# Turning q on VectorE instead of TensorE in an attention and channel-mix kernel

## The chip, the cores and the metric

The kernel runs on one core of a Trainium2 chip. Its engines work side by side, each through its own queue in order: TensorE (PE in the profile; PEld are its weight loads), VectorE (DVE), ScalarE (ACT), GpSimd (POOL) and SyncE (SP); the last two mostly issue transfers (DMAs) here. The metric is the device time of one execution in microseconds (us). The kernel before takes 208.34 us, the median of 3 runs (207.24 to 208.76).

## The reference, cut to what matters

Eight batches, 8 heads, 576 tokens, head size 64, 32 memory slots. Per batch and head the keys and values are pooled into 32 memory rows by a softmax of `phi`, the queries attend to these rows, and the result goes, heads side by side, into a channel mix of width 512 (1024 inside):

```python
a = softmax(phi)                                  # over the 32 slots
k_m = einsum('bhsm,bhsd->bhmd', a, k); v_m = einsum('bhsm,bhsd->bhmd', a, v)
attn = softmax(q @ k_m.T / sqrt(64)) ; x = attn @ v_m   # x: batch, token, 512
x_prev = x shifted by one token (zeros first)
xk = mu_k * x + (1 - mu_k) * x_prev ; xr = mu_r * x + (1 - mu_r) * x_prev
out = sigmoid(xr @ w_r) * (relu(xk @ w_k)**2 @ w_v)
```

## The kernel before, in words

All products run in bf16 with sums in f32. `q`, `k`, `v` and the weights are cast by their loads, which GpSimd issues; `phi` comes as f32. A batch is loaded with 128 partitions as (2 groups of four heads) x (64 rows), and each partition holds 9 tokens of each of four heads (`NJ` = 9, `QR` = 64): token 9 p + j lies in partition p at place j. So a batch's 576 tokens are nine blocks of 64. In the kernel before, all that follows holds the blocks in the order `JT` (even ones, then odd ones), and `store` writes them back to their place.

An attention batch is made of small steps, each a closure in `attention(b)` under a short name:

- `exp`, `z`: exponentials of `phi` (line 225), their sums on PE (247) and the reciprocal `rz`. `kv`, `k`, `v`: pooled keys and values on PE, 36 or 72 small matmuls (237). `nk`, `hn`, `nv`: scaling by `rz`, out of PSUM (274, 281). `tk`, `ht`: the scaled keys are transposed on PE and copied to `kmT` by DVE (301, 305).
- q must have the head dimension on partitions before scores can be made. Batch 0 does this in `qh0`, `qh1` (`tr_q_rows`, 326: 18 transposes for each half of the rows, then one copy out of PSUM by DVE and one by ACT, 329). Batches 1 to 4 do it in `q0`, `q1` (`tr_q`, 339: 36 transposes on PE and four copies out of PSUM, 343; in batch 1 two of the copies go to ACT). Batches 5 to 7 use `qx` (`cross_q`, 315): two DMA transposes of q each, issued by SP, whose queue also issues the stores. After that of batch 5, `hold` puts a tiny copy of GpSimd's behind it, ahead of the later loads.
- `s0`, `s1` (`scores`, 358 and 362): for each group of four heads, eight matmuls of 64 rows by 32 columns with 320 or 256 tokens, into two PSUM tiles (`HALVES`), then two exponentials by ACT into `e`.
- `l0` to `l3` (`denom`, 372 and 377): sums over slots by one matmul, and the logarithm by ACT. `h*z`, `r*z` (382): exp of minus that. `y*`, `w*` (389): the product `at` on DVE.
- Batches 0 and 1 then make xk and xr directly (`nk0` to `nr1`, `mk*`, `mr*`: scaled values 432, matmuls `mxps` 288, copies out 449; `load_mu_b`, named `mub`, makes the `mu_m` they need). From batch 2 on, `x*` makes x (288, 401), `dd` its difference to the token before (413), and `k*d`, `r*d` mix them on DVE (423, 424). `before` says where a block of tokens finds its predecessor.

The channel mix runs over chunks of tokens: `c0` (576 tokens, two parts a and b) to `c8` with `keys` (520 PE, relu by ACT 524, square by DVE 528), `g:t` (`gate`, 543: tile t of 128 tokens, exponential by ACT 548) and `o:t` (`value`, 565; product with the gate on DVE 567, store by `store` on SP). Gates are held in pairs of tiles: after the odd tile, `gate` itself finishes the pair with ln(1 + x) and exp(-x) over 1024 columns (550, 551). Two pairs fit in SBUF.

The order is written out by hand in `PLAN`, one list of words for all engines: each word runs its step's instructions into the engines' queues at that point. `p:` words are loads of batch 0, of batch 1 and of the weights, `b:load` loads batch b + 2 in the order of `LOADS` into the buffers that batch b used; at most eight of GpSimd's loads are under way. All PSUM tiles come from one pool of eight. `busy` steps are idle matmuls.

Of the kernel before, what the change touches and what calls it, by code (L numbers as in the profile page):

```python
# [11 lines left out]
BF16 = mybir.dt.bfloat16  # L12
AF = mybir.ActivationFunctionType
# [5 lines left out]
    "p:q:0a 0:exp1 0:exp0 0:z 0:k0c p:q:0b 0:hn0 0:qh0 0:ht0 0:qh1 p:k:0b 0:s0 0:mub p:v:0a 0:l0 0:k1c 0:l1 0:hn1",  # L19
    "p:v:0b 0:mu 0:ht1 p:wr:0-4 0:h1z 0:v0c 0:s1 0:v1c p:phi:1 0:h0z 0:y1 0:l2 0:l3 0:nk0 0:y0 0:nk1 0:h3z 0:nr1",  # L20
    "p:wk:4-8 0:h2z 0:busy4 0:nr0 0:y3 0:y2 0:mr1 0:mr0 p:wk:0-4 0:mk1 1:exp g:2 g:0 0:mk0 g:3 1:z c0:2a c0:7b c0:6b",
    "c0:4a c0:1b p:k:1 p:q:1 c0:2b 1:k 1:nk c0:0b c0:7a c0:5b c0:3a c0:1a 1:q0 c0:3b 1:q1 1:tk c0:4b c0:0a 1:s0 p:v:1",
    "1:s1 1:v c0:6a 1:l1 1:nr1 1:l0 c0:5a p:wv:0-2 1:nk0 1:l2 p:wv:2-4 1:nk1 1:nr0 1:h1z 1:l3 0:load 1:y1 1:h2z 1:h0z",
    "1:h3z g:1 1:y3 o:3a o:2a 1:y2 1:y0 o:2b o:3b 1:mk1 o:1b 1:mk0 1:mr0 c1:5 1:mr1 c1:2 2:exp c1:6 c1:3 c1:1 c1:0",
    "1:load 2:z g:4 g:5 2:q1 2:q0 2:kv 2:nk o:0b 2:load o:1a 2:tk 3:exp 2:nv c1:7 2:s1 2:s0 c1:4 2:l2 o:0a 2:l1 3:z",
    "2:l0 2:r0z 2:w0 2:l3 2:r1z 2:w1 o:4 o:5 2:x0 3:kv 3:nk 3:nv g:6 3:tk 3:q0 3:q1 2:x1 2:dd 2:k0d g:7 g:8 3:s0",
    "2:k2d 3:s1 o:6 o:7 3:l0 2:r2d 3:l2 3:load 3:l1 2:r0d 3:l3 3:r1z c2:3 4:exp c2:2 c2:5 3:r0z 3:w1 c2:0 3:w0 c2:4",
    "c2:6 g:10 c2:1 4:z 3:x1 4:kv 4:nk 4:nv c2:7 3:x0 g:11 3:dd 4:q0 4:q1 4:tk 5:exp o:11 g:9 5:qx o:10 5:z 5:kv",
    "3:k0d 4:s1 3:k2d 4:s0 o:9 g:12 4:l3 5:nk 3:r0d 4:l2 c3:2 c3:6 5:nv 4:l0 4:l1 4:r1z 4:w1 c3:3 4:r0z 4:w0 5:tk",
    "c3:7 c3:4 3:r2d c3:0 c3:5 5:s0 5:hold 5:load 4:x1 o:8 c3:1 5:l1 4:x0 4:dd g:13 4:k2d 5:l0 g:14 o:13 4:load o:12",  # L30
    "7:exp 5:r0z 4:k0d g:16 5:w0 g:15 7:z 7:kv 5:s1 c4:5 7:qx c4:1 c4:4 6:qx 4:r0d 7:nv c4:0 c4:3 6:exp 5:l2 7:nk",
# [5 lines left out]
    "c7:4 c8:2 c8:7 g:28 g:29 c8:3 c8:0 c8:5 g:31 o:28 o:29 o:31 7:load g:32 o:30 g:33 g:34 g:35 o:32 o:33 o:34 o:35",  # L37
]

LOADS = {None: ("phi", "k", "v", "q"), 2: ("phi", "k", "q", "v")}  # L40
PRE = "k:0a id:"
SUMS = ()

# [577 lines left out]
```

## Time and profile before

| | |
|---|---|
| median of 3 runs | 208.34 us |
| the profiled execution | 208.79 us, its span 207.0 us |
| PE busy | 192.7 us (93% of the span) |
| ACT busy | 159.4 us (77%) |
| DVE busy | 133.9 us (65%) |
| POOL busy | 29.6 us (14%) |
| PE: keys L520, values L565, gates L543 | 66.9, 65.6 and 34.6 us |
| granted clock, mean | 0.998 |
| HBM read and written | 38.28 and 9.44 MB |

The page comes from one execution. Its span begins and ends with the first and last instruction, and the execution takes some 1.8 us more. Busy times of PE overlap where small tiles run beside each other, so that line sums can exceed what a group holds the engine. A group of instructions is given as line, engine, operation, the tiles written and read, the shape, the count, total busy time and mean, then the idle time just ahead of them and what ended it.

### The profile page before, as it was taken

The page shows a single profiled execution, that of the slowest core. Times are in us where ns is not written, and L with a number is a line of the kernel's source. Part 1 is how long each engine was busy: PE and PEld are TensorE (multiplying, and loading weights), DVE is VectorE, ACT ScalarE, POOL GpSimd, SP SyncE. Part 2 cuts the span into 40 slices and gives each one's busy share as a digit, 9 for nine tenths or more (in the row PEclk, how much of TensorE's full clock was granted, in tenths as well). Part 3 has the DMA queues.
Part 4 walks back from the last instruction along what each step waited for, and adds up shares of the span by engine and source line. Part 5 has one row for each costly group of instructions (what it writes and reads, how often), then busy time and mean ns, then how long its engine had stood idle before and what let it go on. Part 6 is the DMA issues. An engine that isn't in the chain of part 4 may idle for free.

```text
span 207.0 us, 5511 instructions
## 1 busy us (share of the span) xinstructions
PE 192.7 (93%) x2213; PEld 103.6 (50%) x2235; DVE 133.9 (65%) x360; ACT 159.4 (77%) x314; POOL 29.6 (14%) x46
## 2 busy tenths in 40 slices
PE   0489999999999999999999999999999999999992
PEld 0355577745655445544458654444444444444441
DVE  1236455884668996899594969767887856615232
ACT  3246999987968998979899977899968655686570
POOL 7644222201504000007400000000000000000000
PEclk9999999999999999999999999999999999999999
DMA  6999999999999999298999997832060215202525
GB/s 160 178 208 260 207 207 205 261 221 292 209 284 240 262 269 201 61 133 205 187 231 298 198 165 115 189 71 52 0 152 5 51 33 119 54 0 62 135 67 141
DMA packets 31641, 33.06 MB, mean 160 GB/s; under 512 B 9072, under 2 KB 26752, under 8 KB 31616
## 3 DMA queue, kind: packets, MB, share of 16 engines
q0 software_dynamic: 17392, 20.91, 54.2%
q1 hardware_dynamic: 13456, 10.96, 24.5%
q10 hardware_dynamic: 768, 0.85, 1.3%
q8 instruction: 17, 0.28, 0.5%
q14 instruction: 8, 0.07, 0.1%
HBM read 38.28 MB, written 9.44 MB: 231 GB/s over the span
## 4 chain that ended last, share of the span: by engine, by line
PE 89%; DMA 6%; issue 1%; POOL 1%; ACT 1%; DVE 0%; SPq 0%; POOLq 0%; DVEq 0%
PE pk L520 31%; PE pv L565 29%; PE pr L543 15%; DMA q<-in_q_dram 4%; PE kvps L237 3%; PE zps L372 2%; PE mxps L288 2%; DMA qT<-q 2%; PE scps L358 2%; PE nops L288 2%; PE qtps L339 1%; PE idle L195 1%; PE zps L247 1%; PE mub L200 1%; PE qtps L326 1%
## 5 line engine op out<-in xcount | busy, mean ns | idle before, releaser
L520 PE MATMUL pk<-xkT,wk 128*128 128x512 bf16 (+4 forms) x346 | 66.9, 340 | 0.4
L565 PE MATMUL pv<-wv,sq 128*128 128x512 bf16 (+1 forms) x322 | 65.6, 353 | 0.4
L524 ACT ACTIVATE rl<-pk 128x512 bf16<-128x512 f32 (+3 forms) x80 | 41.9, 560 | 9.9 <-PE pk L520 8.7
L528 DVE TENSOR_TENSOR sq<-rl 128x512 bf16<-128x512 bf16 (+5 forms) x104 | 32.3, 340 | 26.0 <-ACT rl L524 25.0
L565 PEld LDWEIGHTS <-sq 128*128 128x128 bf16 x328 | 31.4, 98 | 30.0 <-issue 0.5
L520 PEld LDWEIGHTS <-wk 128*128 128x128 bf16 x352 | 32.9, 98 | 26.5 <-issue 0.5
L567 DVE TENSOR_TENSOR o<-sg,pv 128x512 f32<-128x512 f32 (+1 forms) x41 | 24.9, 619 | 18.9 <-PE pv L565 14.1
L543 PE MATMUL pr<-wr,xrT 128*128 128x512 bf16 x134 | 34.6, 381 | 0.5
L548 ACT ACTIVATE sg<-pr 128x512 f32<-128x512 f32 x36 | 21.3, 611 | 12.3 <-PE pr L543 5.2
L543 PEld LDWEIGHTS <-xrT 128*128 128x128 bf16 x144 | 13.5, 98 | 15.4 <-ACT xrT L449 0.4
L550 ACT ACTIVATE sg<-sg 128x1024 f32<-128x1024 f32 x18 | 19.0, 1057 | 0.6
L551 ACT ACTIVATE sg<-sg 128x1024 f32<-128x1024 f32 x18 | 19.0, 1057 | 0.6
L401 ACT CAST x<-nops 128x320 bf16<-128x320 f32 (+1 forms) x48 | 15.8, 428 | 3.6 <-PE nops L288 3.6
L423 DVE TENSOR_SCALAR mu_d<-diff,mu 128x576 bf16<-128x576 bf16 x48 | 15.5, 364 | 0.1
L389 DVE TENSOR_TENSOR atn<-e,lz 128x576 bf16<-128x576 bf16 (+2 forms) x20 | 12.4, 635 | 4.0 <-ACT lz L382 3.8
L377 ACT ACTIVATE lz<-zps 128x320 f32<-128x320 f32 (+1 forms) x32 | 11.9, 420 | 1.6 <-PE zps L372 1.6
L362 ACT ACTIVATE e<-scps 128x320 bf16<-128x320 f32 (+1 forms) x32 | 11.0, 416 | 1.5 <-PE scps L358 1.5
L382 ACT ACTIVATE lz<-lz 128x576 f32<-128x576 f32 (+2 forms) x20 | 11.6, 600 | 0.2
L413 DVE TENSOR_TENSOR diff<-x 128x1024 bf16<-128x1024 bf16 (+1 forms) x18 | 9.0, 554 | 3.4 <-ACT x L401 3.4
L225 ACT ACTIVATE em<-ph 128x1152 bf16<-128x1152 f32 (+1 forms) x9 | 9.4, 1050 | 2.1 <-DMA ph<-in_phi_dram 2.1
L237 PE MATMUL kvps<-kv,em 64*32 64x128 bf16 (+1 forms) x720 | 9.3, 219 | 1.0 <-DMA kv<-in_k_dram 1.0
L424 DVE TENSOR_TENSOR xkT<-x,mu_d 128x1152 bf16<-128x1152 bf16 x12 | 9.1, 759 | 0.4
(66 smaller groups left out, 140.7 us busy)
## 6 DMA issues: line engine op xcount, KB each, us to landing
out_dram<-o SPq DMA_DIRECT2D x61, 128.0 KB, 2.4
ph<-in_phi_dram POOLq DMA_DIRECT2D x7, 576.0 KB, 20.8
kv<-in_k_dram POOLq DMA_DIRECT2D x7, 576.0 KB, 17.3
q<-in_q_dram POOLq DMA_DIRECT2D x7, 576.0 KB, 21.3
kv<-in_v_dram POOLq DMA_DIRECT2D x7, 576.0 KB, 18.8
out_dram<-o SPq DMA_DIRECT2D x18, 64.0 KB, 5.6
wk<-in_moe_w_k_dram POOLq DMA_DIRECT2D x2, 512.0 KB, 14.7
wv<-in_moe_w_v_dram POOLq DMA_DIRECT2D x2, 512.0 KB, 20.0
```

Source lines behind the costliest of these rows:

```text
L237: nc.tensor.matmul(kvps[c][g * M:(g + 1) * M], lhsT=em[ROWS[c], j, g, :], rhs=kv5[ROWS[c], parts, g, j, :], start=j == 0, stop=j == NJ - 1 ...
L401: nc.scalar.copy(st["x"][:, i, sl], pss[i])
L423: nc.vector.tensor_scalar_mul(t[:, i], st["d"][:, pr + i, :], mu1[:, o:o + 1])
L520: nc.tensor.matmul(pk[:, p0 - lo:p1 - lo], lhsT=wk_sb[:, di, fi * 128:(fi + 1) * 128], rhs=xk_T[:, di, p0 % RING:p0 % RING + p1 - p0], sta ...
L524: nc.scalar.activation(rl, pk, AF.Relu)
L528: nc.vector.tensor_mul(sq[:, fi, p:p + p1 - p0], rl[:, p0 - lo:p1 - lo], rl[:, p0 - lo:p1 - lo])
L543: nc.tensor.matmul(pr, lhsT=xr_T[:, di, c0:c0 + 128], rhs=wr_sb[:, di, :], start=(di == 0), stop=(di == ND - 1))
L548: nc.scalar.activation(sg[:, t % 2], pr, AF.Exp, scale=-1.0)
L550: nc.scalar.activation(sg, sg, AF.Ln, bias=1.0)
L551: nc.scalar.activation(sg, sg, AF.Exp, scale=-1.0)
L565: nc.tensor.matmul(pv[:, cols], lhsT=sq[:, fi, p:p + 128], rhs=wv_sb[:, fi, cols], start=(fi == 0), stop=(fi == NF - 1))
L567: nc.vector.tensor_mul(o[:, cols], gated[t // 2][:, t % 2, cols], pv[:, cols])
```

## The change

- q is turned by DVE, SBUF to SBUF. `turn_q` reads bf16 pairs as 32-bit words and transposes each 32x32 block of them: one instruction for two heads of each group (128 partitions, 576 words), for all batches from 1 on (`q0`, `q1`); in batch 0 one for each half of the rows (64 partitions, 1152 words; `qh0`, `qh1`). The transposes on PE, their copies out of PSUM, `cross_q` and `hold` go.
- A partition then holds a pair's place in the head dimension (32 pairs), for 32 rows of q, with both members of the pair side by side. So `norm_k` writes the keys with even and odd members of the head dimension apart, `tr_k` keeps them as two planes `h`, and `scores` sums over the two planes: matmuls of 32 rows by 32 columns with 288 tokens, four row groups (two head groups, two halves of the 64-row blocks), in four PSUM tiles of 288 columns where both head groups run in one step (`s`), or two tiles for one group (batch 0). The exponentials put the halves back in place: `e` has its nine blocks of 64 tokens in natural order.
- `JT` goes: blocks are in natural order, and `before` and `store` follow.
- The two last passes of a pair of gates are a step of their own, `sg:p` (`settle`), and either tile of a pair may come first.
- `LOADS` has one order for all batches, and `PLAN` is written anew. It also loads k's second half ahead of q in batch 0, and `wk`'s first half ahead of the second and of `wr`.

```diff
-    "p:q:0a 0:exp1 0:exp0 0:z 0:k0c p:q:0b 0:hn0 0:qh0 0:ht0 0:qh1 p:k:0b 0:s0 0:mub p:v:0a 0:l0 0:k1c 0:l1 0:hn1",
-    "p:v:0b 0:mu 0:ht1 p:wr:0-4 0:h1z 0:v0c 0:s1 0:v1c p:phi:1 0:h0z 0:y1 0:l2 0:l3 0:nk0 0:y0 0:nk1 0:h3z 0:nr1",
-    "p:wk:4-8 0:h2z 0:busy4 0:nr0 0:y3 0:y2 0:mr1 0:mr0 p:wk:0-4 0:mk1 1:exp g:2 g:0 0:mk0 g:3 1:z c0:2a c0:7b c0:6b",
-    "c0:4a c0:1b p:k:1 p:q:1 c0:2b 1:k 1:nk c0:0b c0:7a c0:5b c0:3a c0:1a 1:q0 c0:3b 1:q1 1:tk c0:4b c0:0a 1:s0 p:v:1",
-    "1:s1 1:v c0:6a 1:l1 1:nr1 1:l0 c0:5a p:wv:0-2 1:nk0 1:l2 p:wv:2-4 1:nk1 1:nr0 1:h1z 1:l3 0:load 1:y1 1:h2z 1:h0z",
-    "1:h3z g:1 1:y3 o:3a o:2a 1:y2 1:y0 o:2b o:3b 1:mk1 o:1b 1:mk0 1:mr0 c1:5 1:mr1 c1:2 2:exp c1:6 c1:3 c1:1 c1:0",
...
+    "0:exp0 p:k:0b 0:exp1 0:z p:q:0a 0:mu 0:k0c p:q:0b p:v:0b 0:k1c 0:hn0 0:hn1 p:v:0a p:wk:0-4 0:qh0 0:ht0 0:ht1",
+    "0:mub 0:qh1 0:s0 0:l0 0:l1 0:h1z 0:s1 0:h0z p:phi:1 0:v1c 0:nk1 0:v0c 0:y0 0:y1 0:l3 0:l2 0:h2z 0:busy3 0:nr1",
+    "p:wk:4-8 0:nk0 0:h3z 0:y2 0:y3 0:nr0 0:mk0 0:mr0 0:mk1 c0:3a 0:mr1 c0:2a p:wr:0-4 c0:2b p:k:1 c0:1b c0:5b c0:7b",
+    "1:exp c0:6b c0:7a g:3 g:2 c0:0a 1:z c0:4b c0:5a 1:k sg:1 1:nk g:1 1:tk p:q:1 1:q1 1:q0 c0:1a c0:4a c0:0b c0:3b",
+    "1:s p:v:1 c0:6a p:wv:0-2 1:l0 1:l1 1:h0z 1:l2 1:l3 1:v p:wv:2-4 1:h2z 1:nk0 1:nr1 1:nk1 1:y0 1:h1z 1:nr0 1:y2",
+    "1:h3z 1:y1 1:y3 g:0 0:load o:3a o:2a 1:mk1 1:mk0 o:3b c1:0 c1:5 1:mr0 c1:4 c1:2 1:load 2:exp o:2b c1:7 sg:0",
+    "1:mr1 g:5 g:4 sg:2 3:exp o:0b o:1a 2:z 2:kv 2:nk 2:q0 o:1b 2:tk 2:q1 o:0a 2:nv c1:1 c1:3 2:s g:7 c1:6 2:l1 2:l0",
+    "2:l2 2:l3 2:r0z 2:w0 2:r1z 2:w1 3:z o:4 6:load o:5 2:x0 3:kv 3:nk 2:x1 g:6 3:q0 3:q1 3:tk 2:dd 2:load 3:nv g:8",
+    "2:k0d 3:s sg:3 2:k2d o:7 2:r0d 4:exp 2:r2d 3:l1 3:l3 3:load 3:l0 3:l2 o:6 3:r0z c2:2 c2:4 3:r1z 3:w1 3:w0 c2:1",
+    "c2:0 g:11 c2:6 4:q0 g:9 c2:3 4:z 3:x1 c2:7 c2:5 3:x0 4:q1 sg:4 4:kv 4:nk 3:dd g:10 4:nv o:9 5:exp 3:k2d o:8 4:tk",
+    "sg:5 g:12 3:k0d o:10 5:q1 4:s 5:kv 3:r2d c3:5 3:r0d 4:l0 c3:1 5:q0 4:l1 c3:3 4:r0z 4:l2 5:z 5:nk 5:load c3:0",
+    "4:l3 5:nv 4:load c3:2 4:r1z c3:7 g:13 4:w0 sg:6 4:w1 5:tk c3:6 o:11 7:load 4:x0 c3:4 g:14 4:x1 7:q1 7:exp 7:q0",
+    "g:15 sg:7 4:dd o:13 o:12 7:z 5:s 7:kv 4:k0d 6:exp o:14 g:17 5:l2 4:r0d g:16 5:l0 5:l1 7:nk 4:k2d 5:l3 sg:8 5:r1z",
+    "7:nv o:15 6:q0 7:tk 5:w1 c4:2 c4:1 c4:0 c4:6 6:z 5:r0z 6:kv 6:nv 7:s 5:w0 6:nk c4:4 4:r2d c4:3 7:l2 c4:5 c4:7",
+    "7:l1 6:q1 7:l3 5:x0 o:17 5:x1 6:tk 5:dd g:18 g:19 7:l0 6:s o:16 sg:9 6:l1 6:l0 5:k2d 6:r0z 5:k0d 6:w0 5:r0d g:21",
+    "7:r1z o:19 7:r0z 6:l3 7:w1 g:20 6:l2 c5:5 6:r1z 6:w1 c5:1 c5:7 c5:6 5:r2d c5:4 c5:2 7:w0 6:x0 c5:3 c5:0 6:x1",
+    "o:18 7:x0 g:23 6:dd 7:x1 6:k2d g:22 sg:11 6:k0d 7:dd sg:10 7:r0d o:23 o:20 6:r2d o:22 c6:1 g:24 c6:6 7:k0d 7:k2d",
+    "g:25 c6:2 c6:5 c6:0 6:r0d c6:4 c6:3 o:21 c6:7 c7:5 c7:4 c7:2 sg:12 c7:6 g:27 o:25 7:r2d g:26 c7:7 sg:13 o:24",
+    "g:31 o:26 g:30 o:27 c8:7 c7:3 c7:0 g:28 c7:1 sg:15 g:29 c8:1 c8:5 sg:14 o:28 c8:4 o:29 o:31 c8:0 c8:6 g:33 o:30",
+    "c8:2 c8:3 g:35 g:32 sg:16 g:34 sg:17 o:32 o:33 o:34 o:35",
...
-LOADS = {None: ("phi", "k", "v", "q"), 2: ("phi", "k", "q", "v")}
+LOADS = {None: ("phi", "k", "v", "q")}
-JT = (0, 2, 4, 6, 8, 1, 3, 5, 7)
+    PB = QR // 2
...
-        def hold():
-
-            spare = work.tile([1, 2], BF16, name="spare", tag="spare", bufs=1)
-            nc.gpsimd.tensor_copy(spare, st["qT"][0:1, :, 0, 0])
-
         def norm_k(cs=(0, 1)):
 
             def go():
                 if "kbd" not in st:
-                    st["kbd"] = work.tile([128, 2, 2, D], BF16, name="kbd", tag="kbd", bufs=3)
+                    st["kbd"] = work.tile([128, 2, 2, 2, PB], BF16, name="kbd", tag="kbd", bufs=3)
                 for c in cs:
                     nc.vector.tensor_scalar_mul(
-                        st["kbd"][:, c], st["k"][c].unsqueeze(1).to_broadcast([128, 2, D]), st["rz"][:, c:c + 1])
+                        st["kbd"][:, :, c],
+                        st["k"][c].rearrange("m (d h) -> m h d", h=2).unsqueeze(2).to_broadcast([128, 2, 2, PB]),
+                        st["rz"][:, c:c + 1])
...
-                n = len(cs)
-                ps = ps_tile([128, n, 128], BF16, "ktps")
-                for i, c in enumerate(cs):
-                    nc.tensor.matmul(ps[:, i], lhsT=st["kbd"][:, c].rearrange("p h d -> p (h d)"), rhs=identity,
-                                     is_transpose=True, start=True, stop=True, skip_group_check=True)
+                ps = ps_tile([128, 2, 128], BF16, "ktps")
+                rows_ = slice(cs[0] * 64, cs[-1] * 64 + 64)
+                for h in range(2):
+                    nc.tensor.matmul(ps[rows_, h],
+                                     lhsT=st["kbd"][:, h, cs[0]:cs[-1] + 1].rearrange("p c w d -> p (c w d)"),
+                                     rhs=identity, is_transpose=True, start=True, stop=True, skip_group_check=True)
                 if "kmT" not in st:
                     st["kmT"] = work.tile([128, 2, 128], BF16, name="kmT", tag="kmT", bufs=3)
-                nc.vector.tensor_copy(st["kmT"][:, cs[0]:cs[0] + n], ps)
+                nc.vector.tensor_copy(st["kmT"][rows_], ps[rows_])
             return go
 
         def q_tile():
             if "qT" not in st:
-                st["qT"] = work.tile([128, 2, HH * NJ // 2, QR], BF16, name="qT", tag="qT", bufs=3)
+                st["qT"] = work.tile([128, HH, NJ * PB, 2], BF16, name="qT", tag="qT", bufs=3)
...
-        def cross_q():
-            for hg in range(2):
-                nc.sync.dma_start_transpose(out=q_tile()[:, hg],
-                                            in_=qs[b % 2][ROWS[hg]].rearrange("p n d -> p (n d)"))
...
-        def tr_q(i):
-            def go():
-                pss = [ps_tile([128, NJ, QR], BF16, "qtps") for _ in range(2)]
-                for n in range(NJ):
-                    n0 = 2 * (NJ * i + n)
-                    for hg in range(2):
-                        r = ROWS[hg]
-                        nc.tensor.matmul(pss[hg][:, n], rhs=identity[r, r], is_transpose=True,
-                                         lhsT=qs[b % 2][r, n0:n0 + 2, :].rearrange("p n d -> p (n d)"),
-                                         start=True, stop=True, skip_group_check=True)
-                for hg in range(2):
-                    (nc.scalar.copy if b < 2 and hg else nc.vector.tensor_copy)(
-                        q_tile()[:, hg, NJ * i:NJ * (i + 1)], pss[hg])
-            return go
-
-        def scores(c):
+        def turn_q(rows_, gs):
+
+            def go():
+                dst = q_tile()[rows_, gs].rearrange("p g n h -> p (g n h)")
+                src = qs[b % 2][rows_, gs.start * NJ:gs.stop * NJ].rearrange("p n d -> p (n d)")
+                nc.vector.transpose(dst.bitcast(U32), src.bitcast(U32))
+            return go
+
+        def scores(cs):
 
             def go():
                 if "e" not in st:
                     st["e"] = work.tile([128, 2, S], BF16, name="e", tag="e", bufs=3)
-                pss = [half_tile(hf, "scps") for hf in range(2)]
-                for g in (0, 2, 1, 3):
-                    m = slice(g * M, (g + 1) * M)
+                pss = {(c, hf): ps_tile([128, NJ, PB], F32, "scps") for c in cs for hf in range(2)}
+                for h in range(2):
+                    for g in range(HH):
+                        m = slice(g * M, (g + 1) * M)
+                        for c in cs:
+                            for hf in range(2):
+                                r = slice((2 * c + hf) * PB, (2 * c + hf + 1) * PB)
+                                nc.tensor.matmul(pss[c, hf][m].rearrange("p j t -> p (j t)"), lhsT=st["kmT"][r, h, m], rhs=st["qT"][r, g, :, h],
+                                                 start=h == 0, stop=h == 1, skip_group_check=True)
+                for c in cs:
+                    e = st["e"][:, c].rearrange("p (j w t) -> p w j t", w=2, t=PB)
                     for hf in range(2):
-                        n = [NJ * g + j for j in JT[5 * hf:5 + 4 * hf]]
-                        r = ROWS[n[0] % 2]
-                        nc.tensor.matmul(pss[hf][m, :], lhsT=st["kmT"][r, c, m],
-                                         rhs=st["qT"][r, c, n[0] // 2:n[-1] // 2 + 1].rearrange("p j t -> p (j t)"),
-                                         start=True, stop=True, skip_group_check=True)
-                for hf in range(2):
-                    nc.scalar.activation(st["e"][:, c, HALVES[hf]], pss[hf], AF.Exp, scale=scale)
+                        nc.scalar.activation(e[:, hf], pss[c, hf], AF.Exp, scale=scale)
...
-        before = [[(QR, 5 * QR, 5 * QR), (1, QR, 4 * QR)], [(5 * QR, S, 0)]]
+        before = [[(QR, 5 * QR, 0), (1, QR, S - QR)], [(5 * QR, S, 4 * QR)]]
...
-            steps[f"q{i}"] = tr_q(i)
-            steps[f"qh{i}"] = tr_q_rows(i)
+            steps[f"q{i}"] = turn_q(slice(0, 128), slice(2 * i, 2 * i + 2))
+            steps[f"qh{i}"] = turn_q(ROWS[i], slice(0, HH))
...
-            steps[f"s{i}"] = scores(i)
+            steps[f"s{i}"] = scores((i,))
...
-            dst = out[b].rearrange("(p j) d -> p j d", j=NJ)[p0:p0 + n, JT[j], cols]
+            dst = out[b].rearrange("(p j) d -> p j d", j=NJ)[p0:p0 + n, j, cols]
...
-            if t % 2 == 0:
+            if t // 2 not in gated:
                 gated[t // 2] = work.tile([128, 2, Dm], F32, name="sg", tag="sg", bufs=2)
             sg = gated[t // 2]
             nc.scalar.activation(sg[:, t % 2], pr, AF.Exp, scale=-1.0)
-            if t % 2 == 1:
-                nc.scalar.activation(sg, sg, AF.Ln, bias=1.0)
-                nc.scalar.activation(sg, sg, AF.Exp, scale=-1.0)
         return go
 
-    def value(t, hs=(0,), n=1):
+    def settle(p):
+
+        def go():
+            nc.scalar.activation(gated[p], gated[p], AF.Ln, bias=1.0)
+            nc.scalar.activation(gated[p], gated[p], AF.Exp, scale=-1.0)
```

## The prediction

> **What bounds the kernel now.** The page was read first: busy shares, then the chain that ended last.
>
> ```profile
> PE 192.7 (93%) x2213; PEld 103.6 (50%) x2235; DVE 133.9 (65%) x360; ACT 159.4 (77%) x314; POOL 29.6 (14%) x46
> PE 89%; DMA 6%; issue 1%; POOL 1%; ACT 1%; DVE 0%; SPq 0%; POOLq 0%; DVEq 0%
> ```
>
> TensorE (PE) is busy for 93% of the span and is 89% of the chain. To see whether that holds everywhere, I took the busy time of each engine in stretches of 10 us (columns: stretch and its length, then PE, PEld, DVE, ACT, POOL busy us with counts, granted clock, DMA share, GB/s):
>
> ```profile
> 30.00:40.00 10.00, 9.95 (x190) 7.58 (x189) 6.71 (x24) 9.50 (x25) 2.98 (x4) 1.00 1.32 232
> ...
> 120.00:130.00 10.00, 9.60 (x151) 4.74 (x150) 7.82 (x21) 7.14 (x16) 0.00 (x0) 1.00 0.94 136
> ...
> 140.00:150.00 10.00, 9.93 (x53) 4.43 (x54) 8.24 (x18) 9.87 (x21) 0.00 (x0) 1.00 0.11 27
> ```
>
> From 30 to 200 us PE is idle for only about 1.6 us in all, and 0.40 of that is in 120 to 130. So a PE microsecond removed there is a microsecond of the end, unless a new wait takes its place. ScalarE (ACT) is the one to watch: 9.5 of 10 us in 30 to 40, 9.87 in 140 to 150. Before about 19 us PE waits for loads and for the short chain of batch 0; after 203.2 us only the last product and store are left.
>
> The chain in order of time (start, length, what) shows what the q transposes hold on PE, beside two other groups of small tiles for scale:
>
> ```profile
> 27.93 0.68 PE kvps L237 x72
> ...
> 31.22 0.37 PE qtps L339 x18
> ...
> 32.13 0.37 PE qtps L339 x18
> ...
> 50.86 0.63 PE qtps L339 x36
> ...
> 63.69 0.63 PE qtps L339 x36
> ...
> 66.49 0.39 PE scps L358 x12
> ...
> 81.23 0.63 PE qtps L339 x36
> ```
>
> The timeline of PE has the start of batch 0 and the only visible wait for a DMA transpose of q:
>
> ```profile
> 10.99 1.14 PE L326 MATMUL qtps<-identity,q 64*128 64x64 bf16 x18 [0.83 <-DMA q<-in_q_dram]
> ...
> 15.80 0.46 PE L358 MATMUL scps<-qT,kmT 64*32 64x320 bf16 x4
> ...
> 19.11 2.30 PE L288 MATMUL mxps<-atn,vm 32*64 32x256 bf16 x56
> ...
> 130.10 0.33 PE L358 MATMUL scps<-qT,kmT 64*32 64x320 bf16 x8 [0.45 <-DMA qT<-q]
> ```
>
> **Removed.** Batches 1 to 4 lose their transposes on PE: 0.37 + 0.37 + 3 x 0.63 = 2.63 us, all inside the dense stretch: -2.63. Batches 5 to 7 lose six DMA transposes on SP; their price on the path is the 0.45 us wait at 130.10: -0.45. With them go two SP waits for q (5.2 us of queue time) and the POOL copy of `hold`, which stood 28.1 us before the later loads. Stores and loads behind them start earlier, but no PE wait names either, so I count nothing. The PSUM copies go too: 16 on VectorE (DVE), 14 x 0.45 + 2 x 0.46 = 7.2 us, and 4 on ACT, 2.6 us, all before 33 us.
>
> **The turn on DVE.** There is no row of a 32x32 turn, so its price is bounded by rows of the same length:
>
> ```profile
> L389 DVE TENSOR_TENSOR atn<-e,lz 128x576 bf16<-128x576 bf16 x12 | 9.0, 756 | 2.4 <-ACT lz L382 2.2
> ...
> L343 DVE COPY qT<-qtps 128x576 bf16<-128x576 bf16 x14 | 5.5, 450 | 1.3 <-PE qtps L339 1.2
> ...
> L389 DVE TENSOR_TENSOR atn<-e,lz 128x256 bf16<-128x256 bf16 x4 | 1.7, 420 | 0.7 <-ACT lz L382 0.7
> ```
>
> The product's slope is (756 - 420) / 320 = 1.05 ns a column over 150 ns fixed, one column per cycle. One turn takes 576 pairs (batches 1 to 7, two each) or 1152 (batch 0, two on 64 rows). Lower bound: the copy's row, 0.45 and about 0.8 us. Upper: two cycles a pair, 1.36 and 2.6. [...] DVE: 14 x 0.76 + 2 x 1.36 = 13.4 us added, 7.2 removed, so 140 of 205 us. That is hidden by its idle third, except in batch 0.
>
> **Start.** Now q's second half lands at 10.95, its transposes and copies follow, PE walks on to the second scores at 15.8 and mixed values start at 19.11. After, k's second half is loaded ahead of q, so by the same landing times (7.3, 8.7, 10.95, 12.3) q's first half is there at 10.95. Turn to 12.4, behind it on DVE two copies of kmT (0.22 each) and, ahead of the second turn, two copies for mu_m (0.42 + 0.41): second turn 13.7 to 15.05. First scores 12.65, their exponentials (0.42 each) by 13.95, denominators and logarithms to 15.3, one reciprocal to 15.7. Second scores are done at 15.55, exponentials by 16.5, logarithms by 17.8, the last two reciprocals by 18.7, so mixed values can begin near 18.8: -0.3. At the turn's lower bound ACT's queue sets nearly the same time (-0.7); at the upper it is +1.3. The weights are loaded in another order (wk's first half, phi 1, wk's second, wr): by position they land at 17.8, 21.7 and 24.2, and the new order asks for wk's second half and wr near 23 and 25. Covered by 1 us or so; without that cover, up to 1 us.
>
> **Scores.** Now 16 matmuls a batch (64 rows deep, 320 or 256 wide): 0.35 to 0.55 us, about 0.38. After: 32 matmuls, 32 deep, 288 wide, four row groups into four PSUM tiles. The width costs 288 / 2.4 = 120 ns at the rate of the 512-wide groups (0.86 us for four); 16 at a time that is 0.24, and eight at a time, as L237 and L358 already run, 0.48. [...] The row decides: kvps issues 72 weight-and-matmul pairs in 0.68 to 0.73 us, 10 ns each, so 32 take 0.32 plus the last one's 0.12. The tokens are also read in steps of two elements, one plane of each pair, which no row shows: full rate if reading isn't the limit, half rate otherwise (eight at a time 0.96, +4.1). I take full rate, since 0.44 already leaves room for sixteen tiles at half rate (0.48): +0.4 over seven warm batches. Ends: -0.7 (0.28) and +4.1.
>
> **Order anew.** `norm_k`, `tr_k`, `diff` and `mixed` keep their number and size of instructions; token order only changes store addresses: nothing. Exponentials become four of 288 columns: by 439 and 393 ns for 320 and 256, 416 each, the same sum. `settle` moves the two 1057 ns ACT passes without changing their number. Loads behave as now to 61 us (each lands 20 us after issue, in order); for batch 2, v goes ahead of q, whose landing near 49 precedes its turn. New is that both halves of a batch's scores run as one step, and a denominator needs both exponentials of its half. In batch 1 only one 320-wide key group (0.54 us) stands between scores and first denominator, against 0.83 us of exponentials and then another pair; ACT has no slack there, so PE waits some 0.6 us; behind it on PE are batch 1's values and g:0, and all that follows. +0.6, ends 0 and +1.6. DVE's turn of batch 7 may stand up to 2 us for q's load (about 12 us after k's issue, with some 10 us of PE work till then); queued behind it are the `diff` of batch 4 and the products of o:13 and o:12. PE has g:15, o:13, o:12 and their PSUM buffers as cover: nothing, at most +1.
>
> **Sum.** -2.63 - 0.45 - 0.3 + 0.4 + 0.6 = -2.4 us. The profiled execution took 208.79 us (span 207.0 and 1.8 around it), so 206.4; the median, 208.34, is 0.45 lower: 205.9. The remaining 1.1 us of small PE gaps can shrink as well as grow with a new order; since ACT loses 2.6 us in the stage where it is tightest, I take 0.3 of them: 205.6.
>
> **Rivals.**
> [...]
> *Slower, 210.5: ACT stands between whole-batch scores and denominators.* If a settle pair (2.11 us) is still ahead of the four exponentials, PE reaches the first denominator after one 1.73 us group and waits 2.11 + 0.83 + 0.1 - 1.73 = 1.3 us. In four of the six batches 1, 2, 3, 4, 6, 7: +5.2 on 205.3. It decides from about 3 us, or 0.5 us a batch. For: ACT at 9.5 and 9.87 of 10. Against: the settle steps of pairs 3 and 9 stand behind the scores near them, and pair 5's is 2.6 us of PE work ahead.
> *More gained, 203.8.* Sixteen tiles at a time (-1.1) and no wait in batch 1 (-0.6).
>
> **Chances.** The sum 0.50, gain spent 0.23, slower 0.18, more gained 0.09. A measurement here tells 1% (2.1 us) from nothing. Under 206.26 lie the last case and most of the first: 0.54; above 210.4, most of the slower one: 0.18; between, 0.28. The range goes from 203.6 to 209.9: below it little of the last case, above it most of the slower one.
>
> **What would show it.** No qtps groups; 16 turns at 0.76 and 1.36 us; a batch's scores near 0.44 us on PE; first mixed values near 18.8; PE idle of 1 us or less at batch 1's denominators, none over 0.5 later; DVE near 140 us. It is wrong if the turn is over 1.3 us, if PE waits for exponentials in several batches, or if loads hold DVE near batches 7 and 6 long enough to reach PE.

## The result: 0.5% faster, a good third of what the sum gave

The changed kernel takes 206.84 us (median of 20 runs, 205.95 to 208.42); the kernel before, run beside it, takes 207.84 us (20 runs, 207.24 to 208.82). The ratio is 0.9947 (0.993 to 0.9963). So it is faster, by 1.0 us, where the prediction had 2.4 us by its parts and 2.7 with the small gaps. That lies within the 1% bound set there, though the interval over twenty runs leaves 1 out.

The profiled execution took 206.84 us, its span 205.1. The page of the changed kernel: busy shares, and the chain that ended last.

```profile
PE 188.7 (92%) x2161; PEld 99.0 (48%) x2184; DVE 138.4 (67%) x360; ACT 155.8 (76%) x310; POOL 29.4 (14%) x45
PE 60%; DMA 21%; issue 7%; DVE 6%; POOL 3%; ACT 2%; POOLq 0%; DVEq 0%
```

PE lost 4.0 us of busy time and DVE gained 4.5 (6.2 in the forecast). The chain is another one: PE was 89% of it before, and now is 60%, with 21% for DMA. By the page's next line 13% are loads of q, of batch 0 (6.9 us) and of batch 6 (18.8 us from 95.00 on), each of which ends a wait of DVE's turn; 8% are one load of keys (62.4 to 79.0 us), for which GpSimd's queue of loads waited.

The groups of the changed kernel by shape have the two new operations (count, then busy us and mean ns, then idle time before them and what ended it):

```profile
L318 DVE STREAM_TRANSPOSE qT<-q 128x576 uint32<-128x576 uint32 x14 | 10.5, 763 | 3.0 <-DMA q<-in_q_dram 3.0
L318 DVE STREAM_TRANSPOSE qT<-q 64x1152 uint32<-64x1152 uint32 x2 | 2.7, 1373 | 0.9 <-DMA q<-in_q_dram 0.8
L333 PE MATMUL scps<-qT,kmT 32*32 32x288 bf16 x256 | 4.7, 310 | 1.2 <-DVE kmT L305 0.8 <-DVE qT L318 0.4
```

The turn costs what was taken for it: 763 and 1373 ns against 0.76 and 1.36 us. Its idle time is new: 3.0 us in which DVE, at the head of its queue, stood for a load of q.

Two stretches in the same columns as before. The first is where PE was busy for 9.95 us of 10, and the second is where the chain runs through q's loads:

```profile
30.00:40.00 10.00, 8.93 (x195) 5.83 (x194) 7.69 (x22) 8.21 (x24) 2.98 (x4) 1.00 1.32 232
110.00:120.00 10.00, 9.20 (x181) 7.04 (x179) 8.11 (x28) 8.24 (x17) 0.00 (x0) 1.00 0.37 96
```

PE's timeline of the changed kernel shows what those stretches hold (start, length, operation; in brackets the idle time ahead and what ended it):

```profile
17.57 2.55 PE L287 MATMUL mxps<-atn,vm 32*64 32x320 bf16 x64
...
31.62 0.48 PE L333 MATMUL scps<-qT,kmT 32*32 32x288 bf16 x32
...
32.96 0.41 PE L348 MATMUL zps<-e,sumh 128*128 128x320 bf16 x2 [0.20 <-ACT e L338]
33.57 0.41 PE L348 MATMUL zps<-e,sumh 128*128 128x320 bf16 x2 [0.20 <-ACT e L338]
...
114.85 0.80 PE L239 MATMUL kvps<-kv,em 64*32 64x128 bf16 x72
115.58 0.48 PE L333 MATMUL scps<-qT,kmT 32*32 32x288 bf16 x32
116.65 1.91 PE L496 MATMUL pk<-xkT,wk 128*128 128x192 bf16 x16 [0.59 <-ACT rl L500]
```

Batch 1's denominators wait twice for exponentials, as forecast. The largest wait is at 116, for relu. DVE's timeline, and then ACT's, tell why relu was late:

```profile
101.00 1.44 DVE L318 STREAM_TRANSPOSE qT<-q 128x576 uint32<-128x576 uint32 x2 [1.26 <-DMA q<-in_q_dram]
...
113.86 0.78 DVE L318 STREAM_TRANSPOSE qT<-q 128x576 uint32<-128x576 uint32 x1 [1.71 <-DMA q<-in_q_dram]
```

```profile
116.00 0.60 ACT L500 ACTIVATE rl<-pk 128x512 bf16<-128x512 f32 x1 [1.40 <-DVE sq L504]
```

The first turn of batch 6 stands 1.71 us at the head of DVE's queue until q lands at 113.84. The squares of `c4` are queued behind it; relu waits for the buffers that they read, and PE for the PSUM tiles that relu reads.

**Where the time went on PE.** A second profile was taken of each kernel (207.0 us span before, 206.0 after), since records of wide matmuls are missing from the first two (22 of 824 before, 23 after). I added up the time from the start of each matmul to the start of the next, less what the profile shows as idle, from the first mixed value to the end:

| PE time in us, from the first mixed value on | before | after | difference |
|---|---|---|---|
| q transposes, batches 1 to 4 | 2.63 | 0 | -2.63 |
| scores, batches 1 to 7 | 3.15 | 2.95 | -0.20 |
| transposes of keys | 0.99 | 0.79 | -0.20 |
| pooled keys and values, denominators, x (`kvps`, `zps` of `e`, `nops`) | 12.54 | 13.38 | +0.84 |
| keys of the mix and mixed values (`pk`, `mxps`) | 67.83 | 69.15 | +1.32 |
| all else (`pr`, `pv`, sums of `phi`) | 96.56 | 96.37 | -0.19 |
| idle | 1.27 | 1.49 | +0.22 |
| in all | 184.97 | 184.14 | -0.83 |

The removed transposes are gone in full and the scores cost nothing. Two rows give back: the small steps that were only moved (+0.84), and +1.32 in matmuls that neither kernel has more of. This second row is the half-rate stretch at the start. Key matmuls of 320 columns start 0.267 us apart there and 0.135 after it. By the first record of the granted clock, of full rate, it ended at 20.6 us in this execution of the kernel before and at 22.1 in this one of the changed kernel. In the first pair of profiles it was the other way round, 21.9 before and 19.5 after, and there the row differs by 0.1 us only. It varies from execution to execution of either kernel, so most of the 1.32 is scatter and not an effect of the change.

### The profile page after: what moved, and what is told of

Its sections match the earlier page's. It is cut to its first block, busy times and chain, and to the rows that moved or that the text cites. A ratio compares the mean times of both kernels' runs of the same rounds, so it can differ in the third digit from the quotient of the medians.

```text
span 205.1 us, 5393 instructions
## 1 busy us (share of the span) xinstructions
PE 188.7 (92%) x2161; PEld 99.0 (48%) x2184; DVE 138.4 (67%) x360; ACT 155.8 (76%) x310; POOL 29.4 (14%) x45
## 4 chain that ended last, share of the span: by engine, by line
PE 60%; DMA 21%; issue 7%; DVE 6%; POOL 3%; ACT 2%; POOLq 0%; DVEq 0%
PE pv L545 22%; PE pk L496 20%; DMA q<-in_q_dram 13%; PE pr L519 10%; DMA kv<-in_k_dram 8%; DVE qT L318 2%; PE mxps L287 2%; PE kvps L239 2%; DVE sq L504 1%; PE nops L287 1%; PE zps L348 1%; POOL kv L109 1%; PE scps L333 1%; DVE atn L365 1%; POOL kv L112 1%
## 5 line engine op out<-in xcount | busy, mean ns | idle before, releaser
L496 PE MATMUL pk<-xkT,wk 128*128 128x512 bf16 (+4 forms) x345 | 67.8, 340 | 0.9 <-ACT rl L500 0.6
L545 PE MATMUL pv<-wv,sq 128*128 128x512 bf16 (+1 forms) x319 | 66.5, 352 | 1.0 <-ACT xkT L425 0.3
L500 ACT ACTIVATE rl<-pk 128x512 bf16<-128x512 f32 (+3 forms) x80 | 43.0, 561 | 18.6 <-PE pk L496 13.7
L519 PE MATMUL pr<-wr,xrT 128*128 128x512 bf16 x137 | 35.8, 380 | 0.4
L524 ACT ACTIVATE sg<-pr 128x512 f32<-128x512 f32 x36 | 21.9, 610 | 8.0 <-PE pr L519 5.6
L519 PEld LDWEIGHTS <-xrT 128*128 128x128 bf16 x144 | 13.3, 98 | 14.6 <-issue 0.4
L530 ACT ACTIVATE sg<-sg 128x1024 f32<-128x1024 f32 x18 | 19.1, 1062 | 0.2
L318 DVE STREAM_TRANSPOSE qT<-q 128x576 uint32<-128x576 uint32 (+1 forms) x16 | 13.2, 839 | 3.8 <-DMA q<-in_q_dram 3.8
L338 ACT ACTIVATE e<-scps 128x288 bf16<-128x288 f32 x32 | 10.6, 419 | 5.9 <-PE scps L333 5.7
L109 POOL DMA_DIRECT2D kv<-in_k_dram x7 | 5.3, 752 | 33.6 <-PE kvps L239 20.9
L249 PE MATMUL zps<-ones,em 128*128 128x2 bf16 x72 | 3.0, 164 | 7.3 <-ACT em L227 7.3
```

What stands on the lines that cost most here:

```text
L318: nc.vector.transpose(dst.bitcast(U32), src.bitcast(U32))
L496: nc.tensor.matmul(pk[:, p0 - lo:p1 - lo], lhsT=wk_sb[:, di, fi * 128:(fi + 1) * 128], rhs=xk_T[:, di, p0 % RING:p0 % RING + p1 - p0], sta ...
L500: nc.scalar.activation(rl, pk, AF.Relu)
L519: nc.tensor.matmul(pr, lhsT=xr_T[:, di, c0:c0 + 128], rhs=wr_sb[:, di, :], start=(di == 0), stop=(di == ND - 1))
L524: nc.scalar.activation(sg[:, t % 2], pr, AF.Exp, scale=-1.0)
L530: nc.scalar.activation(gated[p], gated[p], AF.Ln, bias=1.0)
```

## Experiments

The ratios are to the kernel before, run beside it on the same chip, with 95% intervals. The changed kernel itself, run again beside the first group, is the yardstick.

> The changed kernel once more, as the base for the runs beside it. Two readings of the smaller gain are to be told apart. Run-to-run: the first pair of profiles (spans 207.0 and 205.1 us) overstates the difference, since the profiled run of before lay 0.95 us over its median; then this profile has about the same idle time of PE (1.1 us between 30 and 40, 0.8 between 110 and 120), and the time stays 0.5% (1.0 us) under before. Disturbed profile: the idle times are not there again, and the ratio moves to 0.99 or lower.

Measured: 207.65 us (before: 208.6), ratio 0.9947 (0.9926 to 0.9968), the same as the first time. Waits of PE over 0.1 us add up to 1.4 us here and to 2.0 in the first profile, so a part of those was of that execution alone.

### Does a PE microsecond count?

The transposes of batches 1 to 4 are put back on PE as dead work: they transpose a tile of zeros, in the steps where q is turned, and nothing reads what they write. The output doesn't depend on them.

```diff
         def turn_q(rows_, gs):
             def go():
...
+                if 1 <= b <= 4:
+                    pss = [ps_tile([128, NJ, QR], BF16, "qtps") for _ in range(2)]
+                    for n in range(NJ):
+                        for hg in range(2):
+                            r = ROWS[hg]
+                            nc.tensor.matmul(pss[hg][:, n], rhs=identity[r, r], is_transpose=True, lhsT=zeros[r, :],
+                                             start=True, stop=True, skip_group_check=True)
```

> The 36 transposes of each of batches 1 to 4 are put back on PE as dead work (on zeros, nothing reads the result, no copy out of PSUM), at the places of the turns; all else is the changed kernel. If PE is the bound and each microsecond removed counts, this costs the 2.6 us that the chain of before showed: about 209.4. If the removed work was hidden (PE waits elsewhere anyway), it costs less than 1.3 us: under 208.1.

Measured: 212.33 us, ratio 1.0177 (1.0149 to 1.0206): 4.7 us over the changed kernel beside it and more than the 2.6 expected. On PE the transposes take 2.74 us, idle time grows from 1.49 to 3.15 and the scores by 0.47. One wait holds most of the rest. The two pieces of the scores of batch 3, in this run's PE timeline:

```profile
67.58 0.47 PE L340 MATMUL scps<-qT,kmT 32*32 32x288 bf16 x29
69.55 0.30 PE L340 MATMUL scps<-qT,kmT 32*32 32x288 bf16 x3 [1.50 <-issue]
```

So PE time counts in full, as the prediction had it: the matmuls other than the scores together took only 0.15 us less to make up for it. The 1.50 us are not a wait for a PSUM tile. They stand between the 29th and the last 3 of 32 matmuls, when all four tiles had been written, and none of the three waits for a semaphore. A load of instructions (16 KB) ran from 67.2 to 68.2 us in this profile, but that PE stood for it is not shown; the cause stays open.

### The two waits that the trace shows

First, batch 5's second turn runs directly behind its first. The idea was that its buffer, and so the loads behind it, would come free earlier (words of `PLAN`, cut):

```diff
-o:10 5:q1 4:s 5:kv 3:r2d c3:5 3:r0d 4:l0 c3:1 5:q0 4:l1
+o:10 5:q1 5:q0 4:s 5:kv 3:r2d c3:5 3:r0d 4:l0 c3:1 4:l1
```

> The second turn of batch 5 moves right behind its first, so that the load of q for batch 7, which waits for that turn (92.06 us), and all loads of batch 6 behind it are issued some 2.9 us earlier. If the turn of batch 6 that waits 1.7 us for its q is what makes PE stand 0.8 us between 116 and 119, that goes and the kernel gains 0.6 to 0.8 us. If PE's wait there is ScalarE's backlog, or is made up later, nothing changes (within 0.3 us).

Measured: 206.88 us, 0.9911 (0.9886 to 0.9935). The turn of batch 6 still stood 1.63 us for q and PE 0.51 us behind it. The edit didn't take the wait away: q of batch 6 was issued at 92.75 us, 2.3 us earlier than in the first profile of the changed kernel, but landed at 114.55, no earlier than there (113.84). The four loads of the batch are issued in a row and land in order, q's last: in that first profile 9.7, 12.4, 14.6 and 18.8 us after their issues from 92.79 to 95.00.

Then one 0.54 us key group is moved from ahead of batch 1's scores to behind them, as cover for the exponentials:

```diff
-1:q1 1:q0 c0:1a c0:4a c0:0b c0:3b 1:s p:v:1 c0:6a
+1:q1 1:q0 c0:1a c0:4a c0:0b 1:s p:v:1 c0:3b c0:6a
```

> One key group (c0:3b) moves from before to behind the whole-batch scores of batch 1, as more work between scores and denominators. If PE's waits between 32 and 36 us are the exponentials of the whole-batch scores, the two waits of 0.2 us go and the kernel gains 0.3 to 0.5 us. If ScalarE's queue as a whole is late there, the key group's relu behind the exponentials only moves the wait to the mixed values (38 us), and nothing is gained.

Measured: 207.11 us, 0.9921 (0.989 to 0.9952). The two waits of 0.20 us became 0.21 ahead of the scores (for the turn, which the group had covered), 0.14 at the denominators, and 0.57 rather than 0.34 us for xkT near 40. Neither time stands clearly apart from the changed kernel's.

A stronger move of the same sort: all loads of batch 6 ahead of those of batch 7.

```diff
-g:10 4:nv o:9 5:exp 3:k2d o:8 4:tk
+g:10 4:nv 4:load o:9 5:exp 3:k2d o:8 4:tk
...
-4:l3 5:nv 4:load c3:2 4:r1z
+4:l3 5:nv c3:2 4:r1z
```

> The loads of batch 6 are issued before those of batch 7: its buffers are free at 79 us, and the DMA queues have little to do from 80 to 88. If the wait of the turn for the q of batch 6 (1.7 us on VectorE at 112) is what delays the squares, the relus and then PE (0.5 + 0.2 us at 117 to 119), those waits go and the kernel gains about 0.7 us over the changed one. If batch 7's loads come later for it, its turn waits more at 101 and the gain is lost or turned round (up to 2 us slower).

Measured: 214.82 us, 1.0321 (1.0281 to 1.0362), some 7.8 us over the changed kernel by the ratios where at most 2 were expected. Now q of batch 7 is the late one. Its turn on DVE, then PE:

```profile
107.80 1.44 DVE L318 STREAM_TRANSPOSE qT<-q 128x576 uint32<-128x576 uint32 x2 [8.50 <-DMA q<-in_q_dram]
```

```profile
105.09 0.21 PE L239 MATMUL kvps<-kv,em 64*32 64x128 bf16 x1 [1.27 <-ACT e L338]
111.34 1.16 PE L239 MATMUL kvps<-kv,em 64*32 64x128 bf16 x71 [6.03 <-DVE o L547]
```

While the turn waits, 8.5 us, DVE starts nothing, and PE stands 7.3 us in all, 6.0 of them until DVE has made its products. The stand costs once more. This run's granted clock, by slices of 5.3 us:

```profile
PEclk9999999999999999999955999999999999999999
```

It is 0.5 from 106.6 to 116.8 us, so that the first 5.4 us of PE's work behind the wait run at half rate. Gates and values of the mix take 2.4 us more than in the second profile of the changed kernel.

In these two cases (1.7 and 8.5 us on DVE) PE stood 0.8 and 7.3 us: some cover is there, about 1 us of it, not the three steps and their PSUM buffers that the prediction had counted on.

### What the turn is worth without the new order

The new code (turn on DVE, 32x32 scores, natural token order) in the order of before: same words, each turn where PE's or the DMA's transposes stood (for batches 5 to 7 behind the step that copies the keys), the gates finished at once, the loads in the old order.

```diff
-LOADS = {None: ("phi", "k", "v", "q")}
+LOADS = {None: ("phi", "k", "v", "q"), 2: ("phi", "k", "q", "v")}
...
-1:tk p:q:1 1:q1 1:q0 c0:1a c0:4a c0:0b c0:3b 1:s
+c0:1a 1:q0 c0:3b 1:q1 1:tk c0:4b c0:0a 1:s0 p:v:1 1:s1
```

> The turn and the 32x32 scores alone: the changed kernel's code in the order of before (the loads too, each pair of gates finished right after its second tile, the turns of batches 5 to 7 behind their tk steps, no DMA transposes, no hold). If the turn's gain was whole (2.6 us of transposes, 0.5 us of wait) and the new order spent it, this is 2.5 to 3 us faster than before (0.986). If the slow stretch to 22 us, waits or the small tiles spend it whatever the order, it comes out at about 0.995, as the changed kernel.

Measured: 208.63 us (before: 207.61), ratio 1.0046 (1.0032 to 1.0061). Slower than before, with 2.63 us less of transposes on PE. Its waits on PE over 0.1 us after the start add up to 3.9 us, against 1.2 in the second profile of before. Of the 2.7 us more, nearly 2.4 stand behind DVE's queue. Waits for weights are 1.1 more (the earlier start, 17.58 us, runs into the largest, near 24 us), and the waits for DMA transposes, 0.9, are gone. Two of those behind DVE:

```profile
32.88 0.51 PE L334 MATMUL scps<-qT,kmT 32*32 32x288 bf16 x32 [1.08 <-DVE kmT L306]
...
130.96 1.46 PE L497 MATMUL pk<-xkT,wk 128*128 128x512 bf16 x6 [0.95 <-DVE xkT L401]
```

And DVE's queue ahead of the first:

```profile
31.02 0.77 DVE L319 STREAM_TRANSPOSE qT<-q 128x576 uint32<-128x576 uint32 x1
...
31.89 0.77 DVE L319 STREAM_TRANSPOSE qT<-q 128x576 uint32<-128x576 uint32 x1
32.58 0.25 DVE L306 COPY kmT<-ktps 128x256 bf16<-128x256 bf16 x1
```

The scores need the copy of the keys, and that is queued behind two turns. Before, those two slots held copies of 0.45 us, half of them in batch 1 on ACT. The same kernel with the keys' transposes and copies ahead of the turns in batches 1 and 4:

```diff
-c0:1a 1:q0 c0:3b 1:q1 1:tk c0:4b
+c0:1a 1:tk 1:q0 c0:3b 1:q1 c0:4b
...
-3:dd 4:q0 4:q1 4:tk
+3:dd 4:tk 4:q0 4:q1
```

> The new code in the old order (208.6 us, 1.0046) with one thing moved: in batches 1 and 4 the step tk stands ahead of the turns, so that the copy of kmT no longer waits behind them in VectorE's queue. If the turn's place in that queue is what spends its gain, PE's wait of 1.08 us for kmT before the scores of batch 1 goes, and the time falls by about 1 us to that of before (1.000). If PE only waits somewhere else instead, it stays at 1.004.

Measured: 208.6 us (before: 207.7), 1.004 (1.0019 to 1.006), the same time. Its PE timeline shows that the wait for the copy has become one for the turn, and one for a weight has grown from 1.00 to 1.36:

```profile
24.63 3.01 PE L497 MATMUL pk<-xkT,wk 128*128 128x320 bf16 x24 [1.36 <-DMA wk<-in_moe_w_k_dram]
32.70 0.31 PE L334 MATMUL scps<-qT,kmT 32*32 32x288 bf16 x4 [0.24 <-DVE qT L319]
33.55 0.49 PE L334 MATMUL scps<-qT,kmT 32*32 32x288 bf16 x28 [0.55 <-DVE qT L319]
```

So the new code is worth nothing in the old order, placed as it was here, and is about 2.1 us faster in the new one (1.0046 to 0.9947). The old code in the new order was not run. How much the order would bring without the turn stays open.

### The gates' own steps

The new order, but each pair of gates is finished right behind its second gate, as before (`sg:p` moved; two of eighteen places):

```diff
-g:3 g:2 c0:0a 1:z c0:4b c0:5a 1:k sg:1 1:nk
+g:3 g:2 sg:1 c0:0a 1:z c0:4b c0:5a 1:k 1:nk
...
-g:9 c2:3 4:z 3:x1 c2:7 c2:5 3:x0 4:q1 sg:4 4:kv
+g:9 sg:4 c2:3 4:z 3:x1 c2:7 c2:5 3:x0 4:q1 4:kv
```

> The changed kernel with each pair of gates finished right after its second tile, as before; the order is otherwise kept. If own steps for the two passes (2.1 us of ScalarE) are part of what the new order gains, this is slower than the changed kernel by 0.5 us or more, with PE waiting for exponentials or relus. If the passes can stand anywhere within some microseconds, nothing moves (within 0.4 us).

Measured: 213.61 us, 1.029 (1.0267 to 1.0312), some 7 us over the changed kernel by the ratios. PE's waits over 0.1 us after the start add up to 6.3 us, against 2.0 and 1.4 in the two profiles of the changed kernel. The two largest at denominators:

```profile
69.66 0.27 PE L349 MATMUL zps<-e,sumh 128*128 128x256 bf16 x1 [0.95 <-ACT e L339]
...
133.74 0.41 PE L349 MATMUL zps<-e,sumh 128*128 128x256 bf16 x2 [1.40 <-ACT e L339]
```

Denominators wait for exponentials that stand on ACT behind 2.1 us of gate passes. This is the mechanism of the slower rival, at about the price put on it (1.3 us a place), in these two places rather than four; other steps wait for the rest. It doesn't happen in the changed kernel because the passes have steps of their own, placed away from the scores.

### The half rate at the start

Eleven idle matmuls ahead of all else, in the changed kernel, then in the kernel before:

```diff
-    "0:exp0 p:k:0b 0:exp1 0:z
+    "0:busy11 0:exp0 p:k:0b 0:exp1 0:z
```

> The changed kernel with eleven idle matmuls (128x512 of zeros) at the very start, in time that PE spends waiting for phi. In the profiles so far every matmul takes twice as long until 20.4 to 22.4 us (a 128x320 key matmul 0.27 us apart, later 0.135), whenever the work begins. If that slow stretch eats the earlier start of the changed kernel (mixed values at 17.6 to 18.6 instead of 19.1), keeping PE busy from 1 us on removes it: 1.5 to 3 us faster than the changed kernel, with full rate from the mixed values on. If PE's waits between 6 and 17 us put it back to half rate, the gain is under 0.5 us.

> The same eleven idle matmuls ahead of the kernel before. It has the same slow stretch till 22 us. If the slow stretch is what hides part of the new start's gain, this one gains less than the changed kernel does from them, so that the distance between the two grows from 1.0 to 1.5 us or more. If both gain the same, the start's gain was not hidden by it, and the missing part of the forecast lies later.

Measured: 206.06 us, 0.9908 (0.988 to 0.9937), and for the kernel before 208.53 us against 207.9, 1.0033 (1.0006 to 1.006). The distance between the two grew to 2.5 us. By what was expected, that would mean that the half rate hides part of the new start's gain; but the half rate wasn't taken away, as the row below shows, and what moved the two apart stays open.

Then idle matmuls in all gaps of the first 17 us of the changed kernel, forty in all:

```diff
-0:z p:q:0a 0:mu 0:k0c p:q:0b
+0:z 0:busy3_a p:q:0a 0:mu 0:k0c 0:busy4 p:q:0b
...
-0:mub 0:qh1 0:s0 0:l0
+0:mub 0:busy5 0:qh1 0:s0 0:busy5_b 0:l0
```

> The changed kernel with idle matmuls at the very start and in every wait of PE up to the mixed values (11, 3, 4, 1, 5, 5, 2, 3 and 6 of 512 columns; each fits its wait if it takes 0.22 us, not if it takes 0.43). The eleven alone gave full rate at 6 us but half again from 8 us on, and little or nothing in time. If PE's waits put the rate back, and if some 4 us of mixed values and first keys at half rate (to 22 us) are what the earlier start is lost to, the rate now stays full and the time falls by 1.5 to 2.5 us against the changed kernel (about 205). If the rate still falls back, the idle matmuls delay the start and it gets slower by 1 us or more.

Measured: 206.26 us (before: 207.61), 0.993 (0.9911 to 0.9949). The granted clock by slices of 5 us, first with eleven, then with forty:

```profile
PEclk9755999999999999999999999999999999999999
```

```profile
PEclk9999999999999999999999999999999999999999
```

With eleven, PE has the full rate from 4.3 to 7.7 us and then not until 21.4; the row even shows the stretch, which the row of the changed kernel itself doesn't. With forty the full rate lasts from 5.9 us on. The mixed values begin at 18.21, no earlier than without, but the last idle matmul starts at 17.9 right ahead of them, so the run doesn't tell what sets their start. The gain of 1.5 to 2.5 us that a kept full rate was expected to bring didn't come: both intervals overlap the changed kernel's (0.9926 to 0.9968), so what the half-rate stretch is worth isn't resolved here.

### The three edits together

The edits of the two waits and the eleven idle matmuls, together:

> The changed kernel with the three edits that each stood a little under it, none of them clear: the second turn of batch 5 behind its first, one key group behind the scores of batch 1, eleven idle matmuls at the start. If each was worth its 0.3 to 0.4% (ratios 0.991 to 0.992 against 0.995), together they give about 0.986 to 0.988 of before, some 205 us. If they were the scatter of the runs, it is 0.992 to 0.995.

Measured: 205.91 us (before: 207.7), 0.99 (0.9872 to 0.9928), the fastest here, and between the two expectations. It stands 0.5% under the changed kernel; its interval just misses the first one of that kernel and touches the second. Each of the three edits alone came to 0.991 or 0.992, so they don't add up, and which of them it is stays open.

The second profile of the kernel before:

> The kernel before once more, for its profile. If the first profile of it was a slow execution (its time lay 0.95 us over the median), this span is near 206 us, and the place of the difference shows. If not, the span is 207 us again, mixed values of batch 0 begin near 19.1 us and PE has 1.7 us of idle time from there.

Measured: 208.73 us for its one time, span 207.0 as in the first profile, though mixed values begin at 18.16 us and not near 19.1. Its numbers are in the table above.

## Why the prediction was off

The sign was right, the size was not: 2.7 us forecast from the median of three runs, 1.0 measured. The level had little part in this: the profiled execution, 208.79 us, lies 0.95 over the median of twenty runs, and I had taken half of that off. Step by step:

- *Removed, -2.63.* Right: the table shows it, and the dead transposes cost at least that. The wait for the DMA transpose, -0.45 (0.30 and 0.57 in two places of the second profile), is gone too.
- *The turn, 0.76 and 1.36 us.* An estimate: the product's row of 756 ns, and its 1.05 ns a column over 150 ns for 1152 columns (what the prediction calls a cycle is that 1.05 ns; no run shows DVE's clock). Right to 1%: 763 and 1373 ns; DVE 138.4 us busy against 140.
- *Scores, +0.4.* Measured -0.2 over seven batches. A batch's 32 matmuls take 0.41 us, 13 ns each (forecast 0.44); before it was 0.45 us in the same reckoning, not 0.38. The 0.41 us are less than the 0.48 that the prediction worked out for reading every second element at half rate with sixteen tiles at once.
- *Start, -0.3.* Mixed values begin at 17.57 and 18.08 us in the two profiles of the changed kernel and at 19.11 and 18.16 in those of before: some 0.8 earlier on average. But they then run at half rate until 19.5 to 22.1 us in either kernel, so part of a microsecond won there is lost again. That part is argued, not measured.
- *Batch 1, +0.6.* Right: 0.4 to 0.75 us of waits from the scores to the first values.
- *q's load for batch 7, "nothing, at most +1".* The "nothing" was wrong and the batch another, though the end of +1 held. DVE stood 1.26 us for batch 7, which was hidden, and 1.71 for batch 6; PE stood 0.5 to 0.8 us behind that in both profiles.
- *Small gaps, -0.3.* Wrong sign. Waits over 0.1 us add up to 2.0 and 1.4 us in the two profiles of the changed kernel, 0.45 and 1.2 in those of before: on average +0.9, which holds the 0.6 of batch 1, the wait for q and the end of the DMA transpose's wait. The prediction had -0.15 for all of these (0.6 - 0.45 - 0.3). And the 1.1 us of gaps from which it took the 0.3 were hardly waits at all: each of the missing records leaves a gap of some 0.05 us in the first profile of before, and the complete second one shows almost none of these.

**The step that failed** is, first, *Order anew* with its "nothing" for steps that keep their number and size. They cost 0.84 us more on PE, and nearly all of it can be named. The scores of before had the tile shape of the pooled keys, 64 rows by 32 columns, and those of the changed kernel don't. Where the two stand together, in the second profile of before:

```profile
85.85 0.80 PE L237 MATMUL kvps<-kv,em 64*32 64x128 bf16 x72
86.43 0.56 PE L358 MATMUL scps<-qT,kmT 64*32 64x320 bf16 x16
```

From the start of 72 pooled values to the start of scores it is 0.58 us here, and 0.73 at 114.85 in the changed kernel, shown above. The last pooled value is followed after 0.008 us where the shape stays and after 0.154 where it changes. All three such places of the kernel in the old order show the 0.154, so it comes with the 32x32 scores. The prediction had put no price on it. Before had two places, undisturbed, where pooled values run into scores of the same shape, the changed kernel none: +0.30. Only one of the two is due to the shape; the other group of pooled values no longer stands ahead of scores in the new order.

A denominator that runs into small tiles takes 0.20 to 0.23 us rather than 0.11 to 0.14; there are three of these now and one before: +0.2. One x between pooled values and wide matmuls, near 63 us, takes 0.53 rather than 0.35: +0.18. Of batch 1's waits, 0.16 us lie under the modelled ends of the matmuls ahead and so count here. In the kernel in the old order, denominators and x are back at 3.53 and 3.12 us (3.88 and 3.38 in the new one): that part belongs to the order.

The second half of the miss is *"hidden by its idle third"*, with the "nothing" for q's load. DVE's share of idle time says nothing of who stands behind the turn in its queue. In the old order PE had 2.63 us less of transposes, and nearly 2.4 us of waits behind DVE's queue took most of that. More waits for weights and 0.8 us more in scores, which run one group of heads at a time there (3.97 us for seven batches, 2.95 where both groups run in one step), took the rest. In the new order 0.5 to 0.8 us behind the turn that waits for q are left.

The sum with the terms as measured: -2.63 - 0.2 - 0.2 + 0.84 + 0.9 (waits, the lost DMA transpose included) = -1.3 us, against -1.0 by the medians. Two terms are left out of it because they nearly cancel: the earlier start, -0.8 on average over both pairs of profiles, and the row of keys and mixed values, +0.7 on average (0.1 and 1.3). That the half rate is what makes them cancel is argued, and that row alone scatters by more than the remaining 0.3.

Of the rivals, *gain spent* (a slow turn or slow scores, put at 207.5) came nearest in time, but neither occurred: the turn took 763 ns for 576 pairs, and the matmuls of the scores 13 ns each. The slower one was right about what ACT can do and wrong that this order lets it. *More gained* didn't come, since batch 1's wait is there.

## What to carry to other kernels

Work moved from the bounding engine to one with idle time was paid here in that engine's queue: 2.63 us off TensorE, nearly 2.4 us of waits behind DVE in the old order. Look at what stands behind the new instruction, and who waits for it, before its idle share; the same code came to +0.5% in one order and to -0.5% in another. A turn that stood 8.50 us for a load at the head of DVE's queue held up everything behind it, and the stand of 6.0 us on TensorE behind it was followed by 5.4 us of work at half rate. When small tiles change their shape, count the places where steps of different shapes meet on TensorE: here 0.154 rather than 0.008 us from pooled values to scores, and 0.20 to 0.23 rather than 0.11 to 0.14 for a denominator ahead of small tiles.

## What the runs showed of the hardware

- DVE transposes 4-byte words in 32x32 blocks at 1.06 ns a column over about 150 ns: 763 ns for 128x576 and 1373 ns for 64x1152. A product of two bf16 tiles has the same slope (1.05). A word holds two bf16, so a pair costs one column; a turn of single elements was not run.
- 32 matmuls of 32x32 tiles with 288 columns, q read with a step of two elements, take 0.41 us, 13 ns each.
- Behind a matmul of a 64x32 tile the next one starts after 0.008 us where it has the same shape and after 0.154 where it is 32x32.
- PE's half rate at the start ended at 21.9 and 20.6 us in the two profiles of the kernel before and at 19.5 and 22.1 in those of the changed one, with PE busy for 53 to 61% of the first 20 us. Key matmuls of 320 columns start 0.267 us apart before that point and 0.135 after it. Between two executions of one kernel it moved by 1.3 us (before) and 2.6 us (changed); what sets it is not shown. Where the granted clock changes more than once, the stretches last 3.41 and 13.65 us (eleven idle matmuls in the changed kernel) or 3.41 and 10.24 (in the kernel before): one, four and three times 3.41.
- While PE stood for 6.0 us between two matmuls, its granted clock fell to half, and stayed there for 10.24 us (the run with the loads of batch 6 first).
